# Early transfers of a recurrence and MoE kernel held back until all but the last 1.4 MB ahead have landed

## The chip, the cores and the metric

One core of a Trainium2 chip runs the whole program. The metric is device microseconds of one execution, as the median of several runs of the same kernel. One further execution was taken with the hardware profiler; all rows below come from it. Engines are named as in the profile: PE (matrix products), PEld (its weight loads), DVE (vector), ACT (scalar functions), POOL (GpSimd), and SP, whose queue issues the transfers, which 16 DMA engines carry out.

## The reference

Two stages follow each other. The first is a gated recurrence for 4 batches of 8 heads over 768 steps with a state of 48 x 48:

```
f = 1 / (1 + exp(-f_logit))
for t in range(S):
    state = f[:, :, t, :, None] * state + einsum('bhd,bhe->bhde', k[:, :, t], v[:, :, t])
    y[:, :, t] = einsum('bhd,bhde->bhe', q[:, :, t], state)
```

The second is a two-layer network over its 3072 tokens of 384 values, with 2048 hidden units:

```
h = x @ w_in
g = h * tanh(where(h > 20, h, log1p(exp(min(h, 20)))))
out = g @ w_out
```

## The kernel before, in words

The recurrence is worked in 24 chunks of 128 steps of one batch (NCH = 24, the batches taking turns). Each chunk needs three inputs from memory: the gate logits (`fl`, or for the first four chunks `ft`, a transposed and shorter copy, into tiles `l`), keys and queries together (`kq`), and values (`vn` into `v`). There are three buffers of each, and for the fourth chunk other tiles are lent (`ob`, `n`). The MoE runs in units of 512 tokens by 128 hidden units. Its weights come as 16 raw blocks (`ww` into `raw`), one per 128 hidden units, and are split by ACT and DVE into a high and a low part (`split_w`). The outputs of a chunk are gathered in `xt`, with a small transfer from SBUF to SBUF that moves the fourth head pair into spare rows.

No loop runs on the chip. A planner (`class Plan`) gets every step with its engine, an estimated cost, what it reads and writes, and for a transfer its size in KB, and lays the steps out in time by list scheduling, with ranks nudged by a fixed list of seeds. `Plan.order` gives each step its planned start, and `Plan.issue` emits the steps in that order, so that each engine has one fixed sequence. It also puts dummy products on PE (`idle`, L376, writing `o` from `state`) into planned gaps up to the first output unit. Waits between engines come from the tiles that the steps share. A transfer waits on SP, and all that stand behind it on SP wait too.

Sizes as the planner counts them: `ft` 197 KB (280 for the first two), `fl` and `v` 262, `kq` 524 (700 for the first), `raw` 786 (`RAW`), `xt` 142. In the plan's time scale the first unit's steps stand around 30 us.

Lines that the text speaks of: L386 raw block, L406 and L408 `ft` and `fl`, L413 and L411 `kq`, L414 `v`, L722 the `xt` transfer; on ACT L388 (first pass over a raw block) and L458 (exponential of a cumulated gate); on DVE and POOL L332 (scaling of keys and queries); on PE L445 (cumulated gates), L561 (state update) and L256 (the MoE's first product). The transfers' landings are reported on eight semaphores in turn, which the order of the program calls DMAHW0 to DMAHW7.

Of the kernel before, what the change touches and what calls it, by code (L numbers as in the profile page):

```python
# [57 lines left out]
RAW = 786  # L58
PADS = 450
ALONE = 3  # L60
SP_ISSUE = 470
SQ_DVE = ()
LOW_DVE = range(16)
# [2 lines left out]
class Plan:  # L66
# [13 lines left out]
    def add(self, engine, cost, issue, reads=(), writes=(), size=0, port=False, lag=None):  # L80

        n = len(self.steps)
        before = {self.writer[r] for r in reads if r in self.writer}
        for w in writes:
            before |= set(self.readers.get(w, ()))
            before |= {self.writer[w]} if w in self.writer else set()
        for r in reads:
            if r[0] in ("at", "h", "o"):
                before |= {b for b in self.readers.get(r, ()) if self.steps[b][0] != engine}
        before.discard(n)  # L90
        for r in reads:
            self.readers.setdefault(r, []).append(n)
        for w in writes:
            self.writer[w], self.readers[w] = n, []
        lag = self.LATENCY[engine] if lag is None else lag
        self.steps.append((engine, cost, issue, before, size, port or engine == "pool", lag))
# [82 lines left out]
        return sorted(range(count), key=lambda i: (self.start[i], i))  # L179

    def issue(self):
        at = self.FREE["pe"]
        for i in self.order():
            engine, cost, issue = self.steps[i][:3]
            if engine == "pe":

                if self.start[i] <= self.start[self.until]:
                    while at + 527.0 < self.start[i]:
                        self.idle()
                        at += 427.0 if at > 6500.0 else 853.0  # L190
                at = self.start[i] + cost
            issue()

# [18 lines left out]
def recurrence_moe_kernel(  # L214
# [11 lines left out]
    nc = tc.nc  # L226
# [61 lines left out]
    with tc.tile_pool(name="work", bufs=1) as pool, tc.tile_pool(  # L288
# [27 lines left out]
        plan = Plan()  # L316
        add = plan.add

        done = 0

        def pairs(name, ps=range(NP)):
            return [(name, p) for p in ps]
# [4 lines left out]
        def thirds(name, ps=range(NP)):  # L327
            return [(name, p, m) for p in ps for m in range(3)]
# [26 lines left out]
        def fill(dst, src, reads, writes):  # L355
            add("pool", T_POOL(2 * D), lambda: nc.gpsimd.tensor_copy(
                dst.rearrange("x s a (r m) -> x s a r m", m=4)[:, :, :, :, 3],
                src.rearrange("x a (r m) -> x m a r", m=4)[:, 0:3]), reads, writes)
# [20 lines left out]
        def split_w(j):  # L379
# [5 lines left out]
            kr, kt = ("raw", j % 2), ("wt", j % 2)  # L385
            add("sp", SP_ISSUE, lambda: nc.sync.dma_start(raw.rearrange("p a b -> p (a b)"), ww[j].bitcast(I32)),  # L386
                (), [kr], RAW)
# [12 lines left out]
        def place(n):  # L400
            return n if n <= NR else (n - NR - 1) % NR

        def load(n):
            i = place(n)
            if n < NS:
                add("sp", SP_ISSUE, lambda: nc.sync.dma_start(short[n], ft[n]), (), pairs(("l", i)), 197 if n > 1 else 280)  # L406
            else:
                add("sp", SP_ISSUE, lambda: nc.sync.dma_start(l_[i], fl[n]), (), pairs(("l", i)), 262)  # L408
            if n == NR:
                for x, name in enumerate("kq"):  # L410
                    add("sp", SP_ISSUE, lambda x=x: nc.sync.dma_start(kq_[i][x], kq[n][:, x]), (), thirds((name, i)), 262)  # L411
            else:
                add("sp", SP_ISSUE, lambda: nc.sync.dma_start(kq_all[i], kq[n]), (), thirds(("k", i)) + thirds(("q", i)), 524 if n else 700)  # L413
            add("sp", SP_ISSUE, lambda: nc.sync.dma_start(v_[i], vn[n]), (), [("v", i)], 262)  # L414

# [48 lines left out]

        def stay_behind(other):
            tc.add_manual_dep(
                nc.tensor.nop().ins, other.ins.name,
                mybir.DependencyInfo(mybir.DependencyClass.Sync, mybir.DependencyReason.DATA),  # L470
                reason="row tiles take turns in a bank",
            )

        def half(e):
            return slice(64 * e, 64 * e + 64)
# [69 lines left out]
        def attn2(n):  # L545
# [26 lines left out]
            if join:  # L572
# [3 lines left out]
                def run():  # L576

                    across = intra(1, 64, True)  # L580
                    for p in range(NP):
                        for x in range(2):
                            if not last:
                                add_to(p, x, 1)
                            back = score(p, 0, x, False)
                    stay_behind(across)
                    for p in range(NP):
                        for x in range(2):
                            add_to(p, x, 0, False)
                            score(p, 1, x)  # L590
                    stay_behind(back)
                    inter(False)
                    intra(0, 64)
# [12 lines left out]
            if n < B:  # L606
                add("act", T_ACT(NP * D, True), lambda: nc.scalar.activation(real(mid), flat[0], AF.Copy),
                    keys[:1], [mk])
                if n == ALONE:
                    fill(spare[1][half(1)], mid[half(1), 2:NP], [mk], [loan[1]])  # L610
# [5 lines left out]
        def attn3(n):  # L616
# [21 lines left out]
            def intra(other, m, opens=False):  # L638

                for a in range(2):  # L640
                    for r in range(0, P, m):
                        for e in range(2):
                            c, p = e ^ other, 2 * a + r // 64
                            c0 = (2 * p + e) * 64 + r % 64
                            one = nc.tensor.matmul(  # L645
                                y[e][r : r + m, a, half(c)], v[half(c), c0 : c0 + m], a_x[e][half(c), p, :],
                                start=(opens and a == 0), stop=True, skip_group_check=True,
                            )
                return one

            def pads():


                vp, mp = spare
                for turn in (1, 0):
                    todo = [[], []]
                    for s in range(NK):
                        e, a = divmod(s, 2)
                        for x in range(2):
                            for c in range(2):  # L660
                                if (c ^ e) == turn:
                                    todo[c].append((e, x, a, c, vp[half(c), s, x], a_x[1][half(c), 2 + x, :]))
                            if (1 ^ e) == turn:
                                todo[1].append((e, x, a, 1, mp[half(1), s, x], q[half(1), 2 + x, half(1)]))
                    if not turn:
                        stay_behind(one)
                    for i in range(max(len(t) for t in todo)):
                        for t in todo:
                            if i < len(t):
                                e, x, a, c, w, moving = t[i]  # L670
                                one = nc.tensor.matmul(
                                    y[e][half(x), a, half(c)], w, moving, start=False, stop=True, skip_group_check=True)

            def outputs():
# [4 lines left out]
                intra(1, 64)  # L679
                if n == ALONE:  # L680
                    pads()

            if n == ALONE:
                fill(spare[0], v.rearrange("x (p e c) -> x p e c", p=NP, e=2)[:, 2:NP, 1], [("v", place(n))], [loan[0]])
# [4 lines left out]
            else:  # L689
                if n == ALONE:  # L690
                    qreads += loan
                add("pe", 1850 if n == ALONE else 900 if first else 1150, outputs, qreads, keys)
                leave(n, y, keys, [])

        def leave(n, y, keys, held):
# [8 lines left out]
            for e in (1, 0):  # L704
                to = NK if n == ALONE else NP
                na = min(to - 2 * e, 2)
# [36 lines left out]
        turns = TURNS + [(g, 0, NF) for g in range(2, NG)]  # L743
# [61 lines left out]
        for u in range(len(units) + LAG):  # L805
            if u < len(units):
# [4 lines left out]
                x, hs, us, gs = g % 2, u % 2, u % 2, u % 3  # L811
# [23 lines left out]
    total = P * NCH * NP  # L835
    good = nc.values_load(flag[0:1, 0:1], min_val=0, max_val=total)
    with tc.If(good < total):
# [3 lines left out]
        with tc.tile_pool(name="slow", bufs=1) as pool, tc.tile_pool(  # L841
            name="slow_psum", bufs=1, space=PSUM
        ) as psum:
            def st(shape, name):
                return pool.tile(shape, F32, tag=name, name=name)
# [45 lines left out]
            with tc.For_i(0, NG, 1) as g:  # L891
                x = st([P, NK, GT], "sx")
# [99 lines left out]
```

## Time and profile before

| | |
|---|---|
| median of 3 runs | 486.76 us (486.6, 486.76, 489.02) |
| profiled execution, its own time | 487.94 us |
| span of its instructions | 486.2 us |
| PE busy | 475.5 us (98%) |
| ACT, DVE, POOL busy | 395.9, 305.6, 133.1 us |
| DMA moved | 57.57 MB, mean 118 GB/s |
| mean granted clock of TensorE | 0.998 |

The span is what lies between the first and the last instruction in the profile; the time of an execution has 1.74 us more. Busy shares are means over a start that is rich in transfers, a long middle and an end.

### The profile page before, as it was taken

Reading aid. Unit: us, or ns where it says so; the run is one execution under the profiler, and the core shown is the slowest. Engines: PE = TensorE matmul, PEld = TensorE weight load, DVE = VectorE, ACT = ScalarE, POOL = GpSimd, SP = SyncE. Lnnn points to the kernel's source line nnn. Section 1 sums busy time; section 2 is a strip of 40 time slices with the busy share of each in tenths; the row PEclk is TensorE's granted clock in tenths of the full one; section 3 lists DMA queues with packets and bytes.
Section 4 is the critical chain, followed back from the end, with each engine's and each line's share of the span. In section 5 each row is a group of like instructions: output and inputs, shape, how many; then the busy total and the mean of one; then the engine's idle time right before and its main releaser. Section 6 shows DMA issues by size and latency. Waiting matters only on the chain.

```text
span 486.2 us, 11794 instructions
## 1 busy us (share of the span) xinstructions
PE 475.5 (98%) x4824; PEld 389.5 (80%) x4824; DVE 305.6 (63%) x523; ACT 395.9 (81%) x722; POOL 133.1 (27%) x125
## 2 busy tenths in 40 slices
PE   8899999999999999999999999999999999999995
PEld 7677778888888888788888888888888888888884
DVE  5799999999966777646637467636545433332221
ACT  7988999999998786887887878877787687778681
POOL 4322300000334232242233232332332323242422
PEclk9999999999999999999999999999999999999999
DMA  8975565534614744624325245213522000100001
GB/s 298 396 274 185 197 239 151 211 127 152 204 40 144 213 130 114 176 66 136 94 50 142 93 115 142 88 34 93 168 47 56 12 12 0 44 22 2 0 1 69
DMA packets 56604, 57.57 MB, mean 118 GB/s; under 512 B 36320, under 2 KB 39776, under 8 KB 56544
## 3 DMA queue, kind: packets, MB, share of 16 engines
q1 hardware_dynamic: 56544, 56.77, 37.5%
q8 instruction: 38, 0.62, 0.6%
q14 instruction: 22, 0.18, 0.1%
HBM read 43.25 MB, written 10.49 MB: 111 GB/s over the span
## 4 chain that ended last, share of the span: by engine, by line
PE 92%; DMA 3%; DVE 1%; SPq 1%; ACT 1%; issue 1%; DVEq 0%
PE h L256 40%; PE o L283 39%; PE at L645 3%; PE at L561 3%; PE at L632 2%; PE at L495 2%; DMA v<-vn 1%; PE o L376 1%; DMA kt<-kd 1%; PE at L527 1%; PE at L713 1%; SPq L536 1%; DMA kd<-inv 0%; DVE n L271 0%; DVE a L508 0%
## 5 line engine op out<-in xcount | busy, mean ns | idle before, releaser
L278 POOL TENSOR_TENSOR gl<-g,gh 128x512 fp32r<-128x512 f32 x80 | 106.1, 1328 | 286.8 <-ACT gh L276 268.2
L256 PE MATMUL h<-xt,wh 128*128 128x512 f32 x576 | 179.2, 392 | 0.0
L275 DVE SCALAR_TENSOR_TENSOR g<-n,half,h 128x512 f32<-128x512 f32 x96 | 71.5, 744 | 85.5 <-ACT n L274 81.2
L256 PEld LDWEIGHTS h<-xt,wh 128*128 128x128 f32 x576 | 106.9, 188 | 22.8 <-DVE g L275 0.4
L283 PE MATMUL o<-gh,wh 128*128 128x512 f32 x288 | 113.5, 394 | 0.0
L256 PE MATMUL h<-xt,wl 128*128 128x512 f32 x288 | 112.2, 390 | 0.0
L283 PE MATMUL o<-gl,wh 128*128 128x512 f32 x288 | 112.2, 390 | 0.0
L283 PE MATMUL o<-gh,wl 128*128 128x512 f32 x288 | 112.2, 389 | 0.0
L271 DVE TENSOR_SCALAR n<-n 128x512 f32<-128x512 f32 x96 | 47.5, 495 | 46.8 <-ACT n L270 46.3
L267 ACT ACTIVATE n<-n 128x512 f32<-128x512 f32 x96 | 60.4, 629 | 19.6 <-DVE n L271 19.1
L270 ACT ACTIVATE n<-h 128x512 f32<-128x512 f32 x96 | 56.6, 591 | 23.9 <-PE h L256 23.1
L276 ACT ACTIVATE gh<-g 128x512 fp32r<-128x512 f32 x96 | 60.2, 627 | 15.3 <-DVE g L275 15.2
L273 ACT ACTIVATE n<-n,ones 128x512 f32<-128x512 f32 x96 | 69.4, 723 | 2.5
L283 PEld LDWEIGHTS o<-gh,wh 128*128 128x128 f32 x288 | 54.0, 188 | 11.6
L283 PEld LDWEIGHTS o<-gl,wh 128*128 128x128 f32 x288 | 54.1, 188 | 11.5 <-POOL gl L278 0.2
L256 PEld LDWEIGHTS h<-xt,wl 128*128 128x128 f32 x288 | 54.1, 188 | 11.4
L283 PEld LDWEIGHTS o<-gh,wl 128*128 128x128 f32 x288 | 54.1, 188 | 10.8
L274 ACT ACTIVATE n<-n 128x512 f32<-128x512 f32 x96 | 60.3, 629 | 2.0
L332 DVE TENSOR_TENSOR kq<-kq,at 128x512 f32<-128x512 f32 (+1 forms) x38 | 25.2, 663 | 3.8 <-ACT at L458 3.1
L450 DVE TENSOR_TENSOR_SCAN cum<-go,l 128x512 f32<-128x512 f32 x20 | 24.9, 1246 | 0.8 <-ACT l L441 0.8
L561 PE MATMUL at<-v,kt 64*64 64x48 f32 x672 | 20.5, 219 | 1.6 <-DMA kt<-kd 0.9
L561 PEld LDWEIGHTS at<-v,kt 64*64 64x64 f32 x672 | 18.2, 135 | 4.4 <-issue 1.7
(135 smaller groups left out, 482.2 us busy)
## 6 DMA issues: line engine op xcount, KB each, us to landing
raw<-ww SPq DMA_DIRECT2D x16, 768.0 KB, 4.7
kq<-kq SPq DMA_DIRECT2D x23, 512.0 KB, 4.4
v<-vn SPq DMA_DIRECT2D x23, 256.0 KB, 5.1
l<-fl SPq DMA_DIRECT2D x20, 256.0 KB, 3.0
out<-ob SPq DMA_DIRECT2D x18, 256.0 KB, 2.3
kd<-inv SPq DMA_DIRECT2D x64, 64.0 KB, 2.2
kt<-kd SPq DMA_DIRECT2D x16, 256.0 KB, 2.7
xt<-xt SPq DMA_DIRECT2D x23, 128.0 KB, 2.6
```

The source lines that it names most:

```text
L256: nc.tensor.matmul(h, w[:, j, a * P : (a + 1) * P], xt[:, :, a, x, :], start=(n == 0), stop=(n == 3 * NK - 1))
L267: ("act", T_ACT(GT), 0, lambda: nc.scalar.activation(n, n, AF.Square))
L270: ("act", T_ACT(GT, True), 0, lambda: nc.scalar.activation(n, h, AF.Exp)),
L271: ("dve", 70 + GT / 1.92, 1, lambda: nc.vector.tensor_scalar(n, n, U_CAP, 1.0, ALU.min, ALU.add)),
L273: ("act", T_ACT(GT, False, 1), 0, lambda: nc.scalar.activation(n, n, AF.Ln, bias=ones)),
L274: ("act", T_ACT(GT), 0, lambda: nc.scalar.activation(n, n, AF.Exp, scale=-1.0)),
L275: ("dve", 662, 0, lambda: nc.vector.scalar_tensor_tensor(g, n, half_, h, ALU.subtract, ALU.mult)),
L276: ("act", T_ACT(GT), 0, lambda: nc.scalar.activation(gh, g, AF.Copy)),
L278: ("pool", T_POOL(GT), 1, lambda: nc.gpsimd.tensor_tensor(gl, g, gh.bitcast(F32), ALU.subtract)),
L283: nc.tensor.matmul(o, w[:, j, m * P : (m + 1) * P], x, start=(first and i == 0), stop=(last and i == 2))
L332: add("pool" if on_pool else "dve", cost, lambda: eng.tensor_tensor(dst, x, y, ALU.mult), reads, writes, port=port)
L561: return nc.tensor.matmul(u[c][half(e), p, :], kt[half(c), p, half(e)], moving, start=start, stop=True, skip_group_check=True,)
```

## The change

Every transfer whose planned start lies before 32 us (`FLOW_END`) gets one more dependency. The planner's sizes are summed along SP's order, and the transfer waits for the landing of the last one whose running sum is at least 1400 KB (`FLOW`) below its own, its own size included. Other transfers and all other instructions stay as they are. `stay_behind` is rewritten in terms of the new `follow` without another effect.

```diff
+FLOW = 1400.0
+FLOW_END = 32000.0
...
     def issue(self):
-        at = self.FREE["pe"]
+        at, sent = self.FREE["pe"], []
         for i in self.order():
...
-            issue()
+            one = issue()
+            if engine == "sp" and self.start[i] < FLOW_END:
+                sent.append((one, (sent[-1][1] if sent else 0.0) + self.steps[i][4]))
+                done = [x for x, total in sent if total <= sent[-1][1] - FLOW]
+                if done:
+                    self.follow(one, done[-1])
...
+        def follow(one, other):
+            tc.add_manual_dep(
+                one.ins, other.ins.name,
+                mybir.DependencyInfo(mybir.DependencyClass.Sync, mybir.DependencyReason.DATA),
+                reason="an order that no tile asks for",
+            )
+
+        plan.follow = follow
```

The sequences of PE, DVE, ACT and POOL are the same, waits included, and so is SP's but for its waits. This is SP's queue at the program's start, before the change, from the third transfer on. The tile that is written stands first, with the semaphores waited for in brackets; the transfers' own landings go to DMAHW0, DMAHW1 and so on in SP's order, so that the third one here reports to DMAHW2, and DMAHW0 is the first `ft` tile's.

```order
L413 DMA kq0_83<-kq 128x1024
L386 DMA raw0_118<-ww 128x1536
L413 DMA kq1_84<-kq 128x1024
L414 DMA v0_86<-vn 128x512
L406 DMA l2_82<-ft 128x384
L414 DMA v1_87<-vn 128x512
L406 DMA ob0_115<-ft 128x384 [waits DMAHW0_49]
L386 DMA raw1_119<-ww 128x1536 [waits DMAHW1_49]
L413 DMA kq2_85<-kq 128x1024 [waits DMAHW2_49]
L408 DMA l0_80<-fl 128x512 [waits DMAHW3_49,Activation_49]
```

From the ninth transfer on each waits for the one eight places ahead. This is the same piece of SP's queue with the change.

```order
L420 DMA kq0_83<-kq 128x1024
L393 DMA raw0_118<-ww 128x1536 [waits DMAHW1_49]
L420 DMA kq1_84<-kq 128x1024
L421 DMA v0_86<-vn 128x512 [waits DMAHW2_49]
L413 DMA l2_82<-ft 128x384
L421 DMA v1_87<-vn 128x512
L413 DMA ob0_115<-ft 128x384 [waits DMAHW3_49,DMAHW0_49]
L393 DMA raw1_119<-ww 128x1536 [waits DMAHW5_49]
L420 DMA kq2_85<-kq 128x1024 [waits DMAHW7_49]
L415 DMA l0_80<-fl 128x512 [waits DMAHW0_49,Activation_49]
```

The first raw block now waits for the second `ft` tile, the first `v` tile for the first `kq` tile, the fourth `ft` tile for the first raw block, the second raw block for the first `v` tile, and so on up to the raw block at SP's row 31.

## Rows read from the trace of the kernel before

**Rows 1.** The page, part 1: busy us, share of the span, instructions.
```profile
PE 475.5 (98%) x4824; PEld 389.5 (80%) x4824; DVE 305.6 (63%) x523; ACT 395.9 (81%) x722; POOL 133.1 (27%) x125
```

**Rows 2.** Busy time by window, the middle from 40 to 100 us.
```profile
core 0: us, PE busy (x) PEld busy (x) DVE busy (x) ACT busy (x) POOL busy (x), PEclk, DMA share, GB/s
40.00:100.00 60.00, 59.51 (x731) 47.87 (x731) 58.89 (x97) 58.58 (x111) 6.52 (x6) 1.00 0.61 202
```

**Rows 3.** The same view, three stretches of the first 42 us.
```profile
2.00:5.00 3.00, 3.00 (x9) 2.28 (x8) 1.62 (x6) 2.00 (x8) 2.83 (x10) 1.00 0.89 245
5.00:30.00 25.00, 22.60 (x475) 17.86 (x473) 19.49 (x35) 21.30 (x53) 8.34 (x10) 1.00 1.03 397
...
37.75:41.25 3.50, 3.34 (x64) 2.50 (x57) 3.32 (x6) 2.52 (x6) 1.44 (x2) 1.00 0.90 289
```

**Rows 4.** Timeline of SP's queue: start us, us, line, transfer.
```profile
2.13 0.43 SPq L386 DMA_DIRECT2D raw<-ww  x1
...
5.33 0.45 SPq L386 DMA_DIRECT2D raw<-ww  x1
6.16 0.34 SPq L413 DMA_DIRECT2D kq<-kq  x1
8.51 0.33 SPq L408 DMA_DIRECT2D l<-fl  x1
...
17.88 0.33 SPq L386 DMA_DIRECT2D raw<-ww  x1
```

**Rows 5.** Issue to landing: raw at 2.13, 5.33, 17.88; fl at 36.72.
```profile
DMA to landing us min/median/max: 6.3/6.3/6.3
DMA to landing us min/median/max: 8.6/8.6/8.6
DMA to landing us min/median/max: 7.4/7.4/7.4
DMA to landing us min/median/max: 2.6/2.6/2.6
```

**Rows 6.** The chain that ended last: start us, us, what.
```profile
3.08 7.28 DMA v<-vn
```

**Rows 7.** Timeline of PE: start us, us, operation [idle before <-releaser].
```profile
10.49 0.68 PE L561 MATMUL at<-v,kt 64*64 64x48 f32 x32 [0.34 <-DMA v<-vn]
...
16.81 0.38 PE L445 MATMUL h<-tri,cum 128*128 128x128 f32 x2 [1.10 <-issue]
...
22.57 0.32 PE L561 MATMUL at<-v,kt 64*64 64x48 f32 x3 [0.16 <-issue]
...
28.74 0.92 PE L376 MATMUL o<-state 128*128 128x256 f32 x3 [0.35 <-issue]
```

**Rows 8.** Timelines of POOL, ACT and DVE, columns alike.
```profile
9.84 1.28 POOL L332 TENSOR_TENSOR kq<-kq,inv 128x512 f32<-128x512 f32 x1 [4.85 <-DMA kq<-kq]
...
14.27 0.92 ACT L388 ACTIVATE wt<-raw 128x768 f32<-128x768 f32 x1
...
17.23 0.60 ACT L458 ACTIVATE inv<-h 128x512 f32<-128x512 f32 x1 [0.90 <-PE h L445]
...
25.80 0.90 ACT L388 ACTIVATE wt<-raw 128x768 f32<-128x768 f32 x1
...
18.69 0.69 DVE L332 TENSOR_TENSOR kq<-kq,h 128x512 f32<-128x512 f32 x1 [1.61 <-ACT h L461]
```

**Rows 9.** DMA queues: whole span; 14.2:14.4, 20:20.2, 26.2:26.4, 30:30.2.
```profile
q8 instruction: 38, 0.62, 0.6%
...
q8 instruction: 1, 0.02, 33.7%
q8 instruction: 1, 0.02, 34.2%
q8 instruction: 1, 0.02, 33.3%
q8 instruction: 1, 0.02, 35.1%
```

More of the change, by code (lines that the diff above doesn't have):

```diff
@@ L463, in prep @@
                 times(False, w, q[:, s], q[:, s], dec, kd, kq, port=False)
-        def stay_behind(other):
[L468 to L472, printed above, removed]
+        def follow(one, other):
[5 more added lines that the diff above has]
+        plan.follow = follow
+        def stay_behind(other):
+            follow(nc.tensor.nop(), other)
         def half(e):
```

## Prediction

> **What bounds the kernel now.** I read the busy times first: PE is busy 475.5 of 486.2 us, every other engine less [rows 1]. In the long middle PE, DVE and ACT all run at 98% or more [rows 2], so whatever lead or delay exists at 40 us is handed on to the end. Any change made before 32 us is therefore worth what it does to PE's order of work in the first 40 us, and not more.
>
> Next I read the stretches of the start. From 5 to 30 us the 16 DMA engines are as good as always busy, at 397 GB/s [rows 3]. SP's queue shows why transfers are so old when they land. The transfer at 8.51 stands 2.35 us behind the one at 6.16, and starts 0.08 us after the raw block issued at 2.13 has landed (2.13 + 6.3 = 8.43) [rows 4, 5]. That block stands eight places earlier on SP, and the order of the kernel before shows a wait of each transfer for the one eight places ahead. So eight transfers in flight are the present cap. At 8.51 these are two kq, two v, two ft tiles, a raw block and an fl tile: 0.524 x 2 + 0.262 x 2 + 0.197 x 2 + 0.786 + 0.262 = 3.01 MB, or 7.6 us of work at 397 GB/s; landings of 7.4 to 8.6 us agree [rows 5].
>
> Then I asked who waits for these transfers. The chain that ended last begins with the first v tile, 7.28 us from issue to landing, and PE stands 0.34 us for it at 10.49; POOL waits 4.85 us for the second kq tile and gets it at 9.84 [rows 6 to 8]. After that PE stands for no transfer up to 30 us. It stands three times for nothing that the profile names ("issue"): 1.10 us before 16.81, 0.16 before 22.57, 0.35 before 28.74, together 1.61 us [rows 7]. Another DMA queue explains them. The queue called instruction moved 38 packets of 0.62 MB, 16 KB each; PE ran 4824 + 4824 = 9648 matmuls and loads, 254 to a packet [rows 1, 9]. Packets ran at 14.2, 20.0 and 26.2; each takes 33 to 34% of 16 engines' time in a 0.2 us window, that is 1.1 us of one engine, and PE goes on 1.4 to 1.5 us after its end (14.2 + 1.1 + 1.5 = 16.8) [rows 7, 9]. So PE ran out of instructions, whose fetch came late through busy DMA engines.
>
> **The change part by part.** No instruction moves; only SP's waits change. Sizes are counted in front of each transfer, and it waits until at most about 1.4 MB, itself included, has yet to land. That replaces a cap of some 3.0 MB by one of 1.4 to 1.9.
>
> *Landings.* What is gone from the queue is waiting time, not work: with the rings kept full, transfers land in the same order at the same rate, only issued some 3 to 4 us later (the raw block of 17.88 near 21). The rings stay full if what is in front covers the time in which a transfer can't move data. An fl tile issued into idle rings took 2.6 us [rows 5]; 0.262 MB at 397 GB/s are 0.66, so 1.94 us are fixed, worth 0.77 MB. For most transfers 0.9 to 1.3 MB stand in front at issue. A raw block is 0.786 MB itself, so less is left: the second one (issued at 5.33 before) waits for the first v tile, with two ft tiles and a v tile in front, 0.656 MB or 1.65 us. The rings run dry for 1.94 - 1.65 = 0.29 us. It then lands at 5.33 + 8.6 + 0.3 = 14.2 instead of 13.93; ACT takes it up at 14.27 [rows 5, 8]. Cost: 0 as things stand, up to 0.3 if ACT is earlier by then; I take 0.15, since part of the gain below comes after it. Another gap of the same size precedes the raw block at SP's row 26; no engine stands for that one before, and I take 0.
>
> *The start.* The first raw block now waits for the second ft tile, with one kq tile (0.524 MB) in front, 1.32 us at 397 GB/s: a gap of up to 0.62 us, which the first v tile and the second kq tile would hand to PE. But between 2 and 5 us the engines moved only 245 GB/s [rows 3], at which 0.524 MB last 2.1 us, more than 1.94. I take 0; the bounds are a loss of 0.62 and a gain of 0.34, PE's whole wait at 10.49 (the dummy products ahead of it stand in PE's order and can't be skipped).
>
> *Instruction fetches.* Bounds of the gain: 0, and all three stalls. If the stalls' ends are when a packet's successor is asked for, it started 3.2 us after (16.81 to 20.0), 3.6 us (22.57 to 26.2), and 1.3 us (28.74 to 30.0), the last as the rings drained [rows 7, 9]. What stands in the rings beyond the 0.77 MB of fixed latency falls from 3.01 - 0.77 = 2.24 MB to 0.6 to 1.1, less than half. If the 1.9 to 2.3 us above the floor of 1.3 shrink likewise, a fetch comes at least 1 us sooner; the row at 30.0 is the nearest to that state. The two short stalls then go, 0.51 us. Of the long one at most 0.90 us count, because ACT, which stood 0.90 us for PE's product then, was busy until 16.33 [rows 8]; DVE's 1.61 us behind ACT shift along. I take 0.55 of it, half of the stall, since I can't see how many packets stand ahead of a fetch inside a DMA engine. Gain 0.51 + 0.55 = 1.06.
>
> Where the gain goes: PE reaches its first MoE products about 1 us sooner, the three busy engines follow, and 40 us onward shifts as a block.
>
> **Sum.** Against the profiled execution: 487.94 - 1.06 + 0.15 = 487.0. That execution lies 1.18 us above the median of the runs shown, 486.76, so the median is predicted at 485.9. With the best ends, 0.34 + 0.51 + 0.90 = 1.75 off, it is 485.0; with the worst of this case, 0.62 + 0.3 lost and nothing gained, 487.7.
>
> A rule that speaks against the gain: the Trainium skill's DMA: Bandwidth & Descriptors (Queues, rings and completion order) says that a DMA engine takes turns between the queues that have work, a packet at a time. By it the fetch, on a queue of its own, would not care how deep the data queue is, and the sum would be 486.8 + 0.0 to 0.15. The trace agrees in part: fetches overtake data transfers of 7 to 8 us, and yet they wait 2 us longer under load.
>
> **Rivals.**
> - *The fetch does not care for depth.* Something else (memory under load, a slow engine) makes fetches late, and the load is as before. Stalls stay at 1.61, landings stay: 486.76 plus 0 to 0.9, about 486.9. For it: rate and share are meant to stay at 397 GB/s. Against it: the wait of 1.3 us at the end of the busy stretch.
> - *The window is too small, slower.* The 16 engines don't finish together; one that is ahead now idles while the slowest one's tail holds the window shut, and new transfers start into half-empty rings. When only an fl tile and a raw block were in flight, 37.75 to 41.25, the engines moved 289 GB/s at a share of 0.90 [rows 3]. The place is the raw block issued at 17.88: it lands at 25.28 and ACT takes it at 25.80, a slack of 0.52 us [rows 4, 5, 8]. It has about 20.3 us of transfers behind it since 5 us. Below 397 x 20.3 / (20.3 + 0.52) = 387 GB/s it comes late, and ACT, in order, stands and PE with it. At a mean of 343, halfway to 289, it is 3.2 us late: 2.7 lost, 1.06 still gained, 488.4. At 289 throughout it is 7.6 us late and the time is about 492.8. Against it: the fl tile and the raw block were alone, whereas here two to five transfers are in flight.
> - *More than the sum.* Tiles land earlier too, because engines running ahead on later tiles no longer take rate from the slow one, and POOL and DVE gain at places where I see no wait of PE. More than 2.4 us would need several of these; below 484.5.
>
> **How the numbers follow.** Chances: my case 0.47, the indifferent fetch 0.30, the small window 0.17, more than the sum 0.06. About 0.5%, 2.4 us, is what a measurement of this kernel tells from no change: faster by that is below 484.3, slower above 489.2. The first two cases lie within, 0.77, and so does the third of the small-window case whose rate stays above some 335 GB/s, about 0.05. So faster 0.06, same 0.82, slower 0.12. Range 484.5 to 489.2: it leaves out the last case and the slower two thirds of the third, 0.18 in all. My own case alone reaches from 485.0 to 487.7.
>
> **What would show it.** In the profile after: SP's raw blocks issued near 10, 21 and 26 us and landing 4 to 5 us later; 5 to 30 us still at 390 GB/s or more; PE's "issue" gaps at the 254-instruction steps shorter or gone, and instruction packets starting 1.5 to 2.5 us after such a step; PE's first MoE product 0.5 to 1.5 us earlier. Wrong would be: a rate below 385 there, an ACT or PE wait for a raw block or for the first v tile longer than 0.5 us, or gaps as before.

## The result, and the profile after

The change made the kernel slower: 495.03 us as the median of five runs (494.19 to 495.68), against 487.65 us for the kernel before in the same comparison. The ratio is 1.0141, with a 95% interval of 1.012 to 1.0162. The profiled execution took 495.49 us with a span of 493.7, against 487.94 and 486.2. That is 7.5 us, all of it in the span. The forecast of 485.9 was wrong, and the time lies above its range of 484.5 to 489.2. In the profile after, the lines that the text named stand 7 to 12 numbers further down: the raw block is L393, `kq` L420, `v` L421, ACT's first pass L395, the state update L573, the MoE's first product L263.

The first view is the busy time by window of the kernel after. It answers to [rows 3].

```profile
core 0: us, PE busy (x) PEld busy (x) DVE busy (x) ACT busy (x) POOL busy (x), PEclk, DMA share, GB/s
5.00:30.00 25.00, 21.18 (x465) 17.15 (x464) 17.56 (x32) 17.87 (x45) 5.76 (x8) 0.93 0.86 285
11.00:14.50 3.50, 2.09 (x78) 2.12 (x81) 2.06 (x5) 1.18 (x4) 1.37 (x2) 0.70 0.60 169
12.00:14.00 2.00, 1.59 (x60) 1.62 (x64) 1.43 (x4) 0.40 (x2) 1.06 (x1) 0.60 0.53 125
14.00:16.00 2.00, 1.92 (x65) 1.65 (x58) 1.87 (x5) 0.96 (x2) 0.51 (x1) 0.54 0.83 293
...
26.00:27.00 1.00, 0.91 (x38) 0.71 (x31) 1.00 (x2) 1.00 (x2) 1.00 (x2) 1.00 0.55 123
32.00:34.00 2.00, 0.00 (x0) 0.00 (x0) 1.04 (x2) 2.00 (x8) 1.27 (x1) 1.00 0.50 128
```

From 5 to 30 us the DMA engines moved 285 GB/s in place of 397, at a share of 0.86 in place of 1.03. From 11 to 14.5 us it was 169, and it fell again to 123 from 26 to 27 and to 128 from 32 to 34. PE's granted clock, 1.00 in that stretch before, shows 0.60 and 0.54 from 12 to 16 us; 0.50 is the level of 1.2 GHz.

SP's queue shows which transfers were held. The columns are those of [rows 4].

```profile
3.74 0.33 SPq L393 DMA_DIRECT2D raw<-ww  x1
...
6.12 0.33 SPq L421 DMA_DIRECT2D v<-vn  x1
...
12.29 0.33 SPq L393 DMA_DIRECT2D raw<-ww  x1
...
24.62 0.33 SPq L393 DMA_DIRECT2D raw<-ww  x1
```

The raw blocks of 2.13, 5.33 and 17.88 [rows 4] are issued 1.6, 7.0 and 6.7 us later. From issue to landing these four took, in the same order:

```profile
DMA to landing us min/median/max: 6.7/6.7/6.7
...
DMA to landing us min/median/max: 6.2/6.2/6.2
...
DMA to landing us min/median/max: 5.6/5.6/5.6
...
DMA to landing us min/median/max: 6.6/6.6/6.6
```

Three of them are younger when they land (less time has passed since their issue), by 0.8 to 3.0 us against [rows 5, 6], and the first is 0.4 us older; none gets back what it was held. The third raw block lands at 24.62 + 6.6 = 31.22 in place of 25.28.

Timelines of PE, ACT and POOL show who stands for them, with the columns of [rows 7]. A sign that the clock has fallen is the length: 32 state updates take 1.11 us at 12.41 and 0.68 at 17.28.

```profile
12.41 1.11 PE L573 MATMUL at<-v,kt 64*64 64x48 f32 x32 [2.73 <-DMA v<-vn]
...
17.28 0.68 PE L573 MATMUL at<-v,kt 64*64 64x48 f32 x32
...
34.05 0.66 PE L539 MATMUL at<-ident,kq 128*128 128x128 f32 x4 [2.58 <-POOL kq L339]
...
40.74 0.70 PE L263 MATMUL h<-xt,wh 128*128 128x512 f32 x2 [0.33 <-DMA xt<-xt]
...
31.24 0.89 ACT L395 ACTIVATE wt<-raw 128x768 f32<-128x768 f32 x1 [2.97 <-DMA raw<-ww]
32.03 0.62 ACT L465 ACTIVATE inv<-cum 128x512 f32<-128x512 f32 x1
...
32.73 1.27 POOL L339 TENSOR_TENSOR kq<-kq,inv 128x512 f32<-128x512 f32 x1 [5.64 <-ACT inv L465]
```

The same places in the kernel before, as far as [rows 7] does not show them:

```profile
14.16 0.68 PE L561 MATMUL at<-v,kt 64*64 64x48 f32 x32
...
34.34 0.81 PE L256 MATMUL h<-xt,wh 128*128 128x512 f32 x2
```

Read it as a relay. The first `v` tile makes PE stand 2.73 us where it stood 0.34 [rows 7]. The third raw block makes ACT stand until 31.24, 5.44 us after its start in [rows 8]; behind it on ACT stands `inv`, the exponential of a cumulated gate, at 32.03, for which POOL waits until 32.73, and for POOL's keys PE stands 2.58 us until 34.05. Against the same operations in the trace before, PE is late by 1.92 us at the first state update (12.41 against 10.49), 3.12 at the second (17.28 against 14.16), 2.6 at the third (24.34 against 21.74), and 6.4 at the first product of the MoE (40.74 against 34.34). The span's 7.5 us are there almost in full by then. PE's three "issue" stalls before 30 us [rows 7] are not in this profile, and PE reaches their places 1.9 to 2.2 us later.

The chain that ended last names the hand-over. Its columns are those of [rows 6].

```profile
1.66 4.44 DMA kq<-kq
6.12 6.16 DMA v<-vn
12.29 5.58 DMA raw<-ww
...
26.04 6.16 DMA v<-vn
...
32.26 5.00 DMA raw<-ww
...
38.80 5.68 DMA raw<-ww
```

Before, one early transfer stood on it. Now a landing releases an issue on SP, and that transfer's landing the next: 1.66 + 4.44 is 6.10, 6.12 + 6.16 is 12.28, 26.04 + 6.16 is 32.20.

What was in the rings at such a hand-over is in the view of the DMA queues: first 0 to 12.3 us, then the data queue from 12.5 to 13, from 13.5 to 14 and from 14.5 to 15 (packets, MB, share of 16 engines).

```profile
DMA packets 1252, 3.08 MB, mean 251 GB/s; under 512 B 137, under 2 KB 628, under 8 KB 1252
...
q1 hardware_dynamic: 13, 0.03, 13.7%
...
q1 hardware_dynamic: 15, 0.08, 81.7%
...
q1 hardware_dynamic: 31, 0.19, 102.3%
```

When the second raw block is issued at 12.29, the transfers ahead of it on SP come to 3.15 MB (three `ft` into `l` and one into `ob`, 0.197 each, two `kq` of 0.524, two `v` of 0.262, a raw block of 0.786), and 3.08 MB have been moved. The plan counts 0.656 MB as still ahead; at most 0.07 MB are. The rings are as good as empty: from 12.5 to 13 us 13.7% of 16 engines is the time of about two. In narrow windows of the same view the raw block's first packet, of 6 KB, is at 13.25, 0.96 us after the issue, and the engines are at 0.19 MB in half a microsecond, 380 GB/s, only from 14.5, 2.2 us after it.

### The profile page after: what moved, and what is told of

Read it like the earlier page. It is cut to its first block, busy times and chain, and to the rows that moved or that the text cites. A ratio compares the mean times of both kernels' runs of the same rounds, so it can differ in the third digit from the quotient of the medians.

```text
span 493.7 us, 11793 instructions
## 1 busy us (share of the span) xinstructions
PE 477.0 (97%) x4824; PEld 390.4 (79%) x4824; DVE 306.2 (62%) x523; ACT 395.5 (80%) x722; POOL 132.9 (27%) x125
## 3 DMA queue, kind: packets, MB, share of 16 engines
HBM read 43.25 MB, written 10.49 MB: 109 GB/s over the span
## 4 chain that ended last, share of the span: by engine, by line
PE 80%; DMA 8%; ACT 5%; DVE 3%; issue 1%; SPq 1%; DVEq 0%; ACTq 0%
PE h L263 36%; PE o L290 35%; DMA raw<-ww 3%; DMA v<-vn 2%; PE at L657 2%; PE at L573 2%; PE at L644 2%; PE at L507 1%; DMA kt<-kd 1%; DMA kq<-kq 1%; ACT n L280 1%; ACT gh L283 1%; ACT n L274 1%; DVE cum L457 1%; ACT n L277 1%
## 5 line engine op out<-in xcount | busy, mean ns | idle before, releaser
L263 PE MATMUL h<-xt,wh 128*128 128x512 f32 x576 | 179.3, 392 | 0.3 <-DMA xt<-xt 0.3
L263 PEld LDWEIGHTS h<-xt,wh 128*128 128x128 f32 x576 | 106.8, 188 | 23.6 <-issue 0.7
L263 PE MATMUL h<-xt,wl 128*128 128x512 f32 x288 | 112.2, 390 | 0.0
L263 PEld LDWEIGHTS h<-xt,wl 128*128 128x128 f32 x288 | 54.1, 188 | 11.4
L573 PE MATMUL at<-v,kt 64*64 64x48 f32 x672 | 20.6, 223 | 4.1 <-DMA v<-vn 2.7
L573 PEld LDWEIGHTS at<-v,kt 64*64 64x64 f32 x672 | 18.4, 139 | 6.9 <-issue 4.9
```

Source lines behind the costliest of these rows:

```text
L263: nc.tensor.matmul(h, w[:, j, a * P : (a + 1) * P], xt[:, :, a, x, :], start=(n == 0), stop=(n == 3 * NK - 1))
L573: return nc.tensor.matmul(u[c][half(e), p, :], kt[half(c), p, half(e)], moving, start=start, stop=True, skip_group_check=True,)
```

## The experiments

Two theories stood at the beginning. **Dry rings**: a transfer held for a landing is issued when the rings hold almost nothing, each such hole costs the bytes not moved, and PE, ACT and POOL inherit them; then the loss must follow the size of the window. **Another cause than the window**: the order of waits on SP by itself (a held transfer blocks those behind it), or PE's cold clock as the main cost; then a wider window would keep most of the loss, or a warm clock take most of it away. All intervals are 95%; "before" is the median of the kernel before on the same chip at the same time. The rate is that of 5 to 30 us in the run's one profiled execution.

| label | what holds | median | before | ratio (interval) | GB/s |
|---|---|---|---|---|---|
| after | the whole change | 495.03 | 487.65 | 1.0141 (1.012 to 1.0162) | 285 |
| start_only | first nine transfers | 489.47 | 487.82 | 1.0032 (1.0017 to 1.0047) | 371 |
| later_only | from the tenth on | 493.44 | 487.82 | 1.011 (1.0079 to 1.0141) | 319 |
| flow2000 | window of 2.0 MB | 488.84 | 487.82 | 1.002 (1.0001 to 1.004) | 362 |
| raw_free | all but raw blocks | 491.26 | 487.82 | 1.0073 (1.0048 to 1.0098) | 305 |
| raw_only | raw blocks alone | 492.77 | 487.92 | 1.0087 (1.0058 to 1.0115) | 304 |
| hold10 | the second raw block alone | 489.18 | 488.32 | 1.0013 (0.9995 to 1.0031) | 365 |
| front1400 | 1.4 MB without its own size | 489.56 | 488.32 | 1.0016 (0.9995 to 1.0038) | 333 |
| flow2600 | window of 2.6 MB | 487.95 | 488.32 | 0.9983 (0.9956 to 1.001) | 379 |
| flow2600_again | the same | 488.1 | 487.92 | 0.9997 (0.998 to 1.0013) | 379 |
| start_warm | start_only, 8 dummies on PE | 490.6 | 488.32 | 1.0058 (1.0034 to 1.0083) | 357 |
| start_warm4 | start_only, 4 dummies | 490.96 | 487.92 | 1.005 (1.0029 to 1.0071) | 328 |

### Where the loss is: the start, or what follows

The rule was kept for the first nine transfers, or for all the others.

```diff
-                if done:
+                if done and len(sent) <= 9:     # start_only
+                if done and len(sent) > 9:      # later_only
```

> Only the first nine transfers are held by the 1.4 MB rule, the others as before. Dry rings (theory 1: when the transfer waited for has landed, what stands in front of the held one has nearly all been moved, so the rings run dry and start again slowly): the first v tile still lands near 12.3 us instead of 10.4, PE is about 2 us late there and works some us at a lower granted clock, but the later holes are gone: 2 to 4 us slower than before. Order on SP (theory 2: what costs is that later, urgent transfers stand behind a held one on SP): little stands behind in this part, under 1 us slower. Cold clock (theory 3: most of the loss is PE's lower clock after its long wait at 10 to 12 us): over 4 us of the 7.4 are here.

> The first nine transfers are as before, the rule holds from the tenth on (the second raw block). Dry rings: holes of 1.5 to 2 us at the raw blocks of places 10, 21 and 26 remain, ACT waits for each raw block, 3 to 6 us slower than before; rate from 5 to 30 us near 320 GB/s. Order on SP: nearly the whole 7.4 us. Cold clock: under 2.5 us slower, with PE's clock full from 8 us on.

The start alone cost 0.32%, the rest alone 1.10%, together 1.42%, as much as the whole change: the two add up. Windows and PE's timeline of start_only:

```profile
5.00:30.00 25.00, 21.46 (x467) 17.14 (x466) 17.93 (x34) 20.26 (x51) 7.22 (x9) 0.93 1.00 371
12.00:14.00 2.00, 2.00 (x82) 2.00 (x81) 1.47 (x4) 0.97 (x3) 0.66 (x2) 0.50 1.05 386
...
11.80 1.10 PE L573 MATMUL at<-v,kt 64*64 64x48 f32 x32 [2.37 <-DMA v<-vn]
16.46 0.68 PE L573 MATMUL at<-v,kt 64*64 64x48 f32 x32
...
18.65 0.38 PE L452 MATMUL h<-tri,cum 128*128 128x128 f32 x2 [0.64 <-issue]
```

PE waits 2.37 us for the first `v` tile, and runs at 1.2 GHz from 12 to 14 us while the rings are full again (386 GB/s). It is 2.3 us late at the second update. In this execution, the fastest of the ten, the kernel takes all of it back (the long stall for instructions shrinks from 1.10 to 0.64 us, and the span is 486.0 us against 486.2). By the median 1.65 us remain, under the 2 to 4 us that dry rings let expect and over the 1 us of the order on SP. So a late start by itself is not what costs 7.4 us.

In later_only the same views show the hole at the second raw block, and no wait longer than 0.47 us for the first `v` tile.

```profile
5.00:30.00 25.00, 22.23 (x471) 17.63 (x469) 17.12 (x32) 19.00 (x48) 5.98 (x8) 1.00 0.90 319
11.00:12.00 1.00, 1.00 (x63) 0.89 (x61) 0.76 (x2) 0.38 (x2) 0.47 (x1) 1.00 0.58 100
...
29.16 0.89 ACT L395 ACTIVATE wt<-raw 128x768 f32<-128x768 f32 x1 [3.31 <-DMA raw<-ww]
31.97 0.66 PE L539 MATMUL at<-ident,kq 128*128 128x128 f32 x4 [2.94 <-POOL kq L339]
```

The relay of the kernel after is complete here (raw block, ACT, POOL, PE), without a cold clock from 5 to 30 us (1.00). That is against the clock as the main cost, and the 5.6 us by which the median rose lie within the 3 to 6 expected of dry rings.

### How wide the window must be

```diff
-FLOW = 1400.0
+FLOW = 2000.0     # flow2000
+FLOW = 2600.0     # flow2600, flow2600_again
```

> The window is 2.0 MB instead of 1.4. Dry rings: a raw block then has at least 1.2 MB in front, holes shrink to under 0.5 us each, rate from 5 to 30 us back above 370 GB/s, within 1.5 us of before either way; PE's stalls for instructions may be shorter than before. Order on SP: as many transfers wait, only for less; 3 to 5 us slower. Cold clock: PE's wait for the first v tile decides, and as that shrinks to under 1 us the loss goes too.

> The window is 2.6 MB. Dry rings: no hole, rate 390 GB/s or more from 5 to 30 us, within 0.5 us of before. If a shallower data queue brings instructions sooner, PE's stalls shrink below 1.6 us in all and the time is up to 1 us below before; if the fetch does not care for depth, they stay between 1.4 and 1.8 us. Order on SP: 1 to 3 us slower.

> The 2.6 MB window once more, in five rounds, since its interval of 0.9956 to 1.001 left open if it is below before. Dry rings with fetches that don't care for depth: no difference, ratio 0.998 to 1.002. Shallower rings bring instructions sooner: 0.997 or less.

The waits remain and sit on the same queue, only for transfers further back, and the loss goes from 1.41% to 0.2% and to nothing, as the rate goes from 285 to 362 and 379 GB/s. That refutes the waits on SP as a cause by themselves and shows the window as the cause. The rates stay under the 370 and 390 GB/s that were expected. flow2600 at first looked 0.17% faster with an interval that reaches 1.001; the longer comparison found 0.9997. No version tried here beats the kernel before. Windows and PE's timeline of flow2000, and then of flow2600, show what became of the hoped-for gain:

```profile
5.00:30.00 25.00, 21.24 (x470) 16.46 (x469) 19.05 (x35) 21.28 (x53) 7.88 (x10) 1.00 0.99 362
...
17.21 0.38 PE L452 MATMUL h<-tri,cum 128*128 128x128 f32 x2 [1.01 <-issue]
```

```profile
5.00:30.00 25.00, 22.19 (x474) 17.79 (x473) 18.46 (x35) 21.20 (x53) 8.04 (x9) 1.00 1.02 379
...
17.78 0.38 PE L452 MATMUL h<-tri,cum 128*128 128x128 f32 x2 [1.57 <-issue]
```

The second profile of 2.6 MB, flow2600_again:

```profile
17.32 0.38 PE L452 MATMUL h<-tri,cum 128*128 128x128 f32 x2 [1.01 <-issue]
```

The stall of 1.10 us [rows 7] is 1.01 at 2.0 MB, and 1.57 and 1.01 at 2.6 MB. Two executions of one kernel differ by more than the windows do, so these profiles show no gain from a shallower data queue.

### Which transfers

```diff
-                if done:
+                if done and self.steps[i][4] != RAW:     # raw_free
+                if done and self.steps[i][4] == RAW:     # raw_only
```

> The 1.4 MB rule as in the change, but the raw blocks of weights are never held (their sizes still count). Dry rings: the deepest holes, ahead of the raw blocks, are gone; rate 360 GB/s or more; 0 to 2 us slower than before. Order on SP: the held small transfers still keep the raw blocks behind them on SP, so at least half of the 7.4 us stays. Cold clock: the first v tile still waits for the first kq tile, so 2 us or more stay.

> The 1.4 MB rule for the raw blocks alone (places 4, 10, 21, 26, 31); all other transfers are held as before. Dry rings: the raw blocks have the thinnest fronts (0.5 to 0.8 MB), so most of the 7.2 us is here, 4 to 6 us slower than before; if instead thin fronts of the other tiles cost as much, it is 2 to 3 us, half of the 7.2 with the other half in the run that frees the raw blocks. Order on SP: the transfers behind a held raw block wait with it, 6 us or more.

Without the holds of the raw blocks half of the loss stays (0.73%), and those holds alone cost 0.87%. The two come to 1.6%, which within the intervals is the whole 1.41%. The raw blocks, whose own size leaves least in front of them, are therefore not the whole matter; in raw_free ACT's wait for the third one, which the rule does not hold, is still 3.11 us, since it stands on SP behind tiles that are held.

```profile
29.87 0.89 ACT L395 ACTIVATE wt<-raw 128x768 f32<-128x768 f32 x1 [3.11 <-DMA raw<-ww]
```

For raw_free the expectation of dry rings missed: 0 to 2 us and 360 GB/s or more were expected, 3.4 us and 305 GB/s were measured, close to what the order on SP let expect. The two go together here: a held tile holds all that stand behind it on SP, and so the rings run dry ahead of a free raw block too. Nor does the rate alone order the losses: later_only lost 1.10% at 319 GB/s, raw_free 0.73% at 305, though their intervals overlap.

### One hold alone

```diff
-                if done:
+                if done and len(sent) == 10:     # hold10
```

> One single transfer is held, the second raw block (place 10), for the first v tile as in the change, with 0.656 MB in front. Dry rings, with a dead time of some 2.9 us as the change's trace suggests: a hole worth 1.2 us, the second raw block lands 3.1 us after the fourth ft tile instead of 1.9, and ACT stands 1 us for it; 0.5 to 1.5 us slower than before. With the prediction's dead time of 1.94 us: a hole of 0.3 us and no change. Order on SP: place 10 delays the issue of all that stand behind it, still within the eight in flight; 1 us or more slower, with later transfers landing late too.

This is the term of 0.29 us by itself: the second raw block waits for the first `v` tile, and nothing else is changed. It is issued at 10.57 and lands at 16.37, 4.34 us after the fourth `ft` tile, where it was 1.89 before. The hole is 2.45 us, twice the 1.2 that were expected from the kernel after. The fourth `ft` tile is issued at 4.83 here and at 4.84 before, and takes 7.2 us in both. The rows are the raw block's issue, the landings of the `ft` tile and of the raw block, two windows, and ACT and PE behind them.

```profile
10.57 0.33 SPq L393 DMA_DIRECT2D raw<-ww  x1
...
DMA to landing us min/median/max: 7.2/7.2/7.2
...
DMA to landing us min/median/max: 5.8/5.8/5.8
...
10.50:12.50 2.00, 1.85 (x96) 1.65 (x96) 1.60 (x6) 1.07 (x3) 0.97 (x2) 1.00 0.62 192
20.00:22.00 2.00, 2.00 (x19) 1.61 (x22) 1.98 (x3) 2.00 (x6) 1.12 (x3) 0.51 0.98 306
...
16.37 0.89 ACT L395 ACTIVATE wt<-raw 128x768 f32<-128x768 f32 x1 [1.84 <-DMA raw<-ww]
...
17.95 0.79 PE L644 MATMUL at<-kq,mid 64*64 64x64 f32 x13 [1.62 <-ACT mid L619]
```

By 10.57 the engines had moved 3.00 MB of the 3.15 ahead, so 0.15 MB, 0.4 us at 397 GB/s, were left, not 1.65 us. Hole and rest together are a dead time of 2.45 + 0.4 = 2.85 us. In the profiled execution PE is 1.70 us late at 38.4 us and 1.23 at 54.8, but the span is only 0.5 us longer. The median is 0.86 us up with an interval that reaches no change. So of one hole of 2.45 us the kernel absorbs most; the several of the whole change it can't.

```diff
-                done = [x for x, total in sent if total <= sent[-1][1] - FLOW]
+                done = [x for x, total in sent if total <= sent[-1][1] - self.steps[i][4] - FLOW]
```

> The 1.4 MB are counted without the transfer's own size, so that every held transfer has at least 1.4 MB in front (3.5 us of work at 397 GB/s). Dry rings with a dead time of 2.9 us: no hole left, rate from 5 to 30 us above 380 GB/s, within 1 us of before. Order on SP: still 3 us or more slower, since as many transfers are held.

With 1.4 MB in front of the transfer, its own size not counted, most of the loss is gone too: 0.16%, with an interval that reaches no change. Its runs scatter more than those of the other versions (486.84 to 492.1), and the profile with 333 GB/s, where over 380 were expected, is that of the slowest of them, so its rate isn't to be set beside those of the table.

### The cold clock

```diff
-                add("pe", 640, update, [("kt", n % 2), ("v", place(n))], keys[: 2 - last])
+                add("pe", 640, lambda: [[idle() for _ in range(8 if n == 0 else 0)], update()], [("kt", n % 2), ("v", place(n))], keys[: 2 - last])
```

This is start_only with eight dummy products (four in start_warm4) ahead of the first state update, to keep PE at work while it waits for the `v` tile.

> As the run that holds only the first nine transfers, with eight more dummy products on PE ahead of the first state update, so that PE is busy while it waits for the first v tile. If PE's slow products from 11.8 to 16 us in that run come from its idle time (granted clock 0.84 from 5 to 16 us), they are back at 0.68 us for 32 and PE is 1 to 1.3 us earlier at its second state update; the median then comes 0.5 to 1.2 us below that run's 489.5. If the clock has another cause, no change.

> As the run with eight more dummy products, with four (8 matmul records of 0.2 to 0.3 us, some 2 us), which end about when the first v tile lands. Clock theory: the first state update takes 0.68 us for 32 products again and the second starts near 15.5 us instead of 16.5 in the run that holds the first nine; median 0.3 to 1.2 us below that run's 489.5. If waits elsewhere take the gain back, equal to it.

The clock did what was wanted. One window of start_warm, then one window and a PE row of start_warm4:

```profile
12.00:14.00 2.00, 2.00 (x47) 1.56 (x49) 0.93 (x2) 0.00 (x0) 0.51 (x1) 1.00 1.00 358
```

```profile
12.00:14.00 2.00, 1.07 (x56) 0.98 (x60) 1.44 (x3) 0.35 (x2) 1.27 (x1) 1.00 0.91 309
...
19.66 0.34 PE L573 MATMUL at<-v,kt 64*64 64x48 f32 x2 [2.39 <-issue]
```

It shows 1.00 in place of 0.50, and the time is not better: 0.58 and 0.50% against 0.32 of start_only. The eight dummies kept PE until 13.4 us, where start_only had the tile at 11.8. With four, PE stood 2.39 us for instructions at 19.66; the added products move the place in PE's program at which a fetch is due, which is the likely reason and not a shown one. As a remedy both missed. They show that a busy PE keeps its clock here; what the clock costs in the kernel after they don't price, since a new stall came with them. That profile of start_warm4 is of its slowest run.

## Why the prediction was wrong

**What bounds the kernel.** Right in its frame: what is lost before 40 us is handed on as a block. PE's 6.4 us at the first MoE product became 7.5 at the end. In hold10's profile, though, most of a lag of 1.70 us was made up after 38 us, so the middle is not quite as rigid as [rows 2] suggested.

**The step that failed: the rings stay full.** The prediction put it as "The rings stay full if what is in front covers the time in which a transfer can't move data", with 1.94 us as that time and the plan's sum as what is in front. Both numbers were wrong in the same direction. What is in front: not 0.656 MB but 0.07 MB (after) and 0.15 MB (hold10), because by the time a landing is told, nearly all that was issued behind it has moved too. The trace points at the slowest engines: from 12.5 to 13 us, just after the landing, some two of 16 still work off what is left, and the others stand. A late report explains little of it. The Trainium skill's DMA: Bandwidth & Descriptors (Anatomy of one DMA — SWDGE (gpsimd) path) states, of GpSimd's transfers, that most of a fixed time of about 2.0 us lies between the last byte and its report. For SP's transfers this trace shows otherwise. The fl tile of [rows 5] has no packet from its issue at 36.72 to 37.75 (the row below); in narrow windows of that view its last one ends at 39.0, and it has landed at 36.72 + 2.6 = 39.3. So about 1.0 us lies ahead of the first packet, and 0.3 behind the last.

```profile
DMA packets 0, 0.00 MB, mean 0 GB/s; under 512 B 0, under 2 KB 0, under 8 KB 0
```

The dead time: taken from a small transfer into idle rings [rows 5], which doesn't say how long the rings take to come back to 380 GB/s; here it was 2.2 us after the issue (after), and counted by the landing the dead time was 2.85 us (hold10). So the hole is 2.45 us (hold10) in place of 0.29. And it is not one hole: in the kernel after the rate falls to 125, 123 and 128 GB/s around three hand-overs (12, 26 and 32 us), and to 285 in place of 397 over 25 us. 20.3 us of transfers at the old rate take 28.3 at the new. Two of the signs of being wrong that the prediction named are there: the rate below 385 GB/s, and waits of PE and ACT over 0.5 us.

**The start, taken as nothing.** "0.524 MB last 2.1 us, more than 1.94. I take 0" failed by the same step. The first `v` tile landed at 12.28 in place of 10.36, and PE's wait grew by 2.39 us, far beyond the bound of 0.62. Alone it was worth 1.65 us.

**The fetch, a gain of 1.06.** It did not come as time. At 2.0 and 2.6 MB, where the rings are nearly full, the long stall is 1.01, 1.57 and 1.01 us, and in flow2000 the fetches start 3.3, 4.4 and 2.6 us after the step before, not 1.3. The indifferent fetch, given 0.30, agrees with these runs. The rule of the Trainium skill's DMA: Bandwidth & Descriptors (Queues, rings and completion order), that an engine takes turns between queues, agrees with these waits. In the kernel after, the fetches start at 21.31, 26.29 and 33.10, which is 2.6, 1.5 and 2.4 us after the same steps, the first two sooner than the 3.2 and 3.6 us before; but PE stood for tiles there, so no gain shows. If nearly empty rings bring a fetch sooner, and what makes it wait under load, stays open.

**The rival that came true** is "The window is too small, slower", given 0.17, with the slowest engine's tail as its mechanism. Its worst price, 492.8 "at 289 throughout", is still 2.2 us short of 495.03, 0.9 of them because the kernel before ran at 487.65 and not at 486.76. Without the gain its formula gives, at the measured 285 GB/s, 20.3 x (397/285 - 1) = 8.0 us late, less the slack of 0.52: 7.5, and the median rose by 7.4. That these agree is in part luck, since the place is only partly right: ACT takes up the third raw block 5.44 us late, and the rest came later, where the chain has the next two raw blocks (32.26 and 38.80); what each of them and the cold clock add, no run separates. The forecast thought the rate of 37.75 to 41.25, 289 GB/s, was that of two transfers alone, and argued from "two to five transfers are in flight" that it wouldn't apply. It was the nearest row there was, and 285 was measured.

**The clock** was in no term. In the kernel after, PE's second update is 1.2 us later still than the first, and between the two the granted clock is 0.60 and 0.54. Before, no wait of PE from 8 to 30 us was over 1.10 us, and the clock was 1.00.

## What to carry to other kernels

A cap on bytes in flight must be judged by what is still unmoved when the landing that it waits for is reported, not by the planned sum: here a window of 1.4 MB left almost nothing, and 2.6 MB were needed to lose nothing. Price a hand-over from a landing to the next issue by a stretch of the trace in which few transfers are in flight (289 GB/s here), since the time of one small transfer understated it. A transfer's age at its landing is not a cost by itself: here transfers landed up to 3.0 us younger, and the kernel was slower.

## What the runs showed that was not expected

- Between an issue into rings that are empty or nearly so and the first packet lies about 1 us: over 1.0 for the fl tile of 36.72 (before), 0.96 for the raw block of 12.29 (after), and 0.97 for that of 10.57 in hold10, whose first packet is at 11.54.
- After an empty stretch the first packets are slow. In the kernel after, 15 packets of 0.08 MB in all took 81.7% of 16 engines from 13.5 to 14 us: 0.44 us for some 5.3 KB. From 14.5 to 15 they took 0.26 us for some 6.1 KB. Per KB that is about twice as long; why, no run here shows.
- A wait of PE of 2.37 us (start_only) or 2.73 us (after) was followed by a granted clock of 0.50 to 0.60 for 2 to 4 us. In hold10 a wait of 1.62 us at 17.95 was followed by 0.51 from 20 to 22 us, after PE had gone on working for some 2 us. Not every such wait was: 2.58 us before 34.05 (after) and 2.94 before 31.97 (later_only) left the clock at 1.00 up to 36 us.
- In the profile with four dummy products more on PE a stall for instructions is 2.39 us long, and in that with eight more the longest is 0.85. That the cost of a fetch depends on the work at the place where it falls due would explain it; no run here shows it.
